# First scores in eight array tiles, and attention placed among the preceding entry's steps, in a fused attention and two-MLP kernel

## The chip, the cores and the metric

The kernel runs on one core of a Trainium2 chip. The metric is the device time of one execution in microseconds (us), the median of three runs. A profiled execution gives the rows; all times are from its trace unless a run is named.

## The reference

Attention in two steps for 8 entries (batch) of 8 heads, 576 tokens and 64 dimensions, with 32 packed queries per head; then an ELU MLP and a second one with SoLU and layer norm. All data are fp32.

```python
def sm_attn(qq, kk, vv):
    s = scale * np.matmul(qq, kk.transpose(0, 1, 3, 2))
    s = s - np.max(s, axis=-1, keepdims=True)
    a = np.exp(s)
    a = a / (np.sum(a, axis=-1, keepdims=True) + 1e-09)
    return np.matmul(a, vv)
p_packed = sm_attn(p, k, v)
out = sm_attn(q, p_packed, p_packed)
...
h = x @ w_in
g = np.where(h > 0.0, h, alpha * (np.exp(np.minimum(h, 0.0)) - 1.0))
return (g @ w_out).astype(np.float32)
```

The second MLP (`_moe2_ref`) multiplies by `w_in2`, takes h times softmax of h, normalises, scales by `g_ln` and multiplies by `w_out2`.

## The kernel before, in words

Weights come as 64-bit words and are narrowed to fp32 on ScalarE and VectorE (`narrow`, four operations per piece of 512 columns); matmuls of the MLPs run in three passes over a high and a low part (`mm3`), so nearly every operand is split into two.

**Attention of entry b.** `s1_mm` gives the first scores (packed queries against k) for a group g of four heads: four matmuls of 128x64, with the packed queries of two heads in a block-diagonal `pt_bd`. `s1_max`, `s1_exp` and `s1_div` are the softmax over 576 keys. For b of 2 and more the probabilities are transposed by `t1_blocks` (32x32 blocks on VectorE) and `t1_move`, 16 block copies per group into `a_sb`; entries 0 and 1 use TensorE (`t1_mm`). `pp_mm` multiplies by v, a group at a time, and `pp_blocks` (16 transposes of 32x32 for both groups) lays the packed values out as `ppT`. `s2_mm` gives the second scores of a half of the tokens, in eight 64x32 tiles of the array (`packed_mm`); a chain of VectorE operations and an exponential on ScalarE are its softmax, and `s2_split` makes the operand `AT`.

**M blocks.** `m_mm` multiplies the packed values by `w_in` in advance: M(b, c) for c of 0 to 3, eight matmuls of 64x32 tiles and 512 columns, split by `m_hi` and `m_lo`. Five slots hold them.

**FFN steps.** 256 steps (b, half, f), f of 0 to 15. A step is `ffn_h` (six matmuls of 288 columns, tile `h`, from `AT` and M(b, f // 4)), `ffn_exp` (two ScalarE operations, tile `fe`), `ffn_max` (VectorE), `ffn_split` (`ghi` on ScalarE, `glo` on VectorE) and `ffn_x2` (12 matmuls of 288 columns into `acc`), three steps behind its `h`. The first 48 steps take entries 0 and 1 in groups of four f, with partial sums through DRAM. From about 766 us on the second MLP runs over 36 blocks of 128 tokens, in a fixed order written at the end of the kernel.

**What sets the order.** Every piece is a `node` with an engine, a cost in us, needs, buffers that it takes and gives back, and perhaps a due time. `order()` computes how late each may start from the due times of its readers, then places nodes one by one: of the nodes of an engine that can start within 0.3 us of the first, the one that may wait least. The result is the program order of TensorE, VectorE, ScalarE and the SP queue; each engine then runs in that order. Due times stand on the steps alone (`FIRST_US + STEP_US * n`), so an entry's attention has no due time of its own. One PSUM tile (two banks, tag `misc`) is shared by all of `s1`, `t1`, `pp`, `s2` and M blocks, so each waits until the one before it is emptied. Costs in the tables are constants, such as

```python
a_in = [node(("mv", *x, h), ACT if h in ACT_MOVES else DVE, 0.75, [("eB", *x), prev_pp],
node(("ppt", *x), DVE, 0.25 if b < 2 else 1.3, [("pp", *x)],
```

where `mv` is four block copies. At the start k, v and weights are loaded in the order of the list `first`; p of entry 0 goes through ScalarE's queue.

Of the kernel before, what the change touches and what calls it, by code (L numbers as in the profile page):

```python
# [34 lines left out]
def attention_mlp_kernel(ctx: ExitStack, tc: tile.TileContext, q, k, v, v_tail, p,  # L35
# [172 lines left out]
    def load_p(b, eng):  # L208
        eng.dma_start(out=pt_bd[0:64, :, 0:NP], in_=p[b, 0:64])
        eng.dma_start(out=pt_bd[64:P, :, NP:], in_=p[b, 64:P])  # L210

    def load_k(b, g, tag=None):
        if tag is None:
            t = work.tile([P, 2, S], F32, tag="k", name=f"k{b}_{g}", bufs=1)
        else:
            t = slot(f"k{b}_{g}", [P, 2, 1024], tag, F32)[:, :, 0:S]
        sp.dma_start(out=t, in_=k[b, g])
        kt[b, g] = t

    def load_v(b, g, tag=None):  # L220
        if tag is None:
            t = v_sb
        else:
            t = slot(f"v{b}_{g}", [P, 8, 4 * D], tag, F32)
            nc.gpsimd.memset(t[S - 4 * CH:, 4], 0.0)
        sp.dma_start(out=t[0:CH, 0:4], in_=v[b, g])
# [808 lines left out]
```

## Time and profile before

| what | value |
|---|---|
| runs (median of three) | 1182.26 us (1179.63 to 1182.43) |
| the profiled execution's own time | 1178.58 us |
| its span, first to last instruction | 1176.8 us |
| TensorE (PE) busy | 1117.9 us, 95% |
| VectorE (DVE) busy | 894.4 us, 76% |
| ScalarE (ACT) busy | 718.6 us, 61% |
| mean granted TensorE clock | 0.987 |
| moved by DMA | 111.04 MB, 94 GB/s |

Busy time of TensorE is modelled, since matmuls overlap: the distance between the starts of two matmuls tells more than a duration. PEld is the loading of weights into the array, which runs beside the matmuls. A releaser (`<-`) is the instruction or transfer that ended a wait. The trace's names leave numbers out: `s` is the first scores (from `k`) and the second ones (from `q`), `h` hidden values of a step, `acc` outputs of a step, `pp` packed values before and `ppT` after the transpose.

### The profile page before, as it was taken

The page shows a single profiled execution, that of the slowest core. Times are in us where ns is not written, and L with a number is a line of the kernel's source. Part 1 is how long each engine was busy: PE and PEld are TensorE (multiplying, and loading weights), DVE is VectorE, ACT ScalarE, POOL GpSimd, SP SyncE. Part 2 cuts the span into 40 slices and gives each one's busy share as a digit, 9 for nine tenths or more (in the row PEclk, how much of TensorE's full clock was granted, in tenths as well). Part 3 has the DMA queues.
Part 4 walks back from the last instruction along what each step waited for, and adds up shares of the span by engine and source line. Part 5 has one row for each costly group of instructions (what it writes and reads, how often), then busy time and mean ns, then how long its engine had stood idle before and what let it go on. Part 6 is the DMA issues. An engine that isn't in the chain of part 4 may idle for free.

```text
span 1176.8 us, 20606 instructions
## 1 busy us (share of the span) xinstructions
PE 1117.9 (95%) x7916; PEld 979.5 (83%) x7916; DVE 894.4 (76%) x2022; ACT 718.6 (61%) x1539; POOL 21.3 (2%) x45
## 2 busy tenths in 40 slices
PE   4699999899999999999999999999999999999997
PEld 2478889699799899899889889988888888888885
DVE  4999995858858868767877765478888788788774
ACT  2567765465465565565466465647766766766674
POOL 0000000000000000000000000000000000000000
PEclk7799999999999999999999999999999999999999
DMA  9837332213322412321422151611111111000000
GB/s 328 333 117 235 121 111 82 84 41 113 101 93 72 145 57 97 119 93 62 132 80 90 46 178 59 218 57 54 54 37 54 52 39 54 27 28 19 28 28 36
DMA packets 53554, 111.04 MB, mean 94 GB/s; under 512 B 8400, under 2 KB 27600, under 8 KB 51664
## 3 DMA queue, kind: packets, MB, share of 16 engines
q1 hardware_dynamic: 52912, 109.66, 27.5%
q8 instruction: 62, 1.02, 0.4%
q14 instruction: 36, 0.29, 0.1%
q10 hardware_dynamic: 544, 0.07, 0.0%
HBM read 77.14 MB, written 32.57 MB: 93 GB/s over the span
## 4 chain that ended last, share of the span: by engine, by line
PE 42%; DVE 31%; ACT 14%; issue 7%; DMA 4%; POOL 1%; SPq 0%; ACTq 0%; POOLq 0%; DVEq 0%
PE acc L64 8%; PE acc L66 8%; PE acc L65 8%; ACT lnX L542 6%; PE h L64 5%; PE h L65 5%; PE h L66 4%; DVE lnB L532 4%; DVE a_sb L295 2%; DVE ln L525 2%; PE m L332 2%; DVE z L517 2%; ACT h L520 2%; DVE lnT L151 2%; DVE nm L508 2%
## 5 line engine op out<-in xcount | busy, mean ns | idle before, releaser
L64 PE MATMUL acc<-ghi,wo 128*128 128x288 f32 x1024 | 308.6, 301 | 1.7 <-ACT x L471 0.7
L66 PE MATMUL acc<-glo,wo 128*128 128x288 f32 x1024 | 302.7, 296 | 1.4 <-DVE glo L434 1.4
L65 PE MATMUL acc<-ghi,wo 128*128 128x288 f32 x1024 | 302.2, 295 | 0.0
L64 PEld LDWEIGHTS acc<-ghi,wo 128*128 128x128 f32 x1024 | 191.9, 187 | 30.8 <-ACT fe L419 14.8
L66 PEld LDWEIGHTS acc<-glo,wo 128*128 128x128 f32 x1024 | 192.6, 188 | 2.6 <-DVE glo L434 2.0
L65 PEld LDWEIGHTS acc<-ghi,wo 128*128 128x128 f32 x1024 | 192.6, 188 | 0.0
L559 PE MATMUL o<-wo,lnT 128*128 128x512 f32 (+1 forms) x592 | 185.5, 386 | 5.6 <-ACT lnT L149 5.6
L424 DVE SCALAR_TENSOR_TENSOR fe<-fe,h 128x288 f32<-128x288 f32 x256 | 114.3, 452 | 88.6 <-ACT fe L419 86.0
L418 ACT ACTIVATE fe<-h 128x288 f32<-128x288 f32 x256 | 104.5, 408 | 118.2 <-PE h L66 92.8
L431 ACT CAST ghi<-fe 128x288 fp32r<-128x288 f32 x256 | 109.4, 431 | 105.2 <-DVE fe L424 104.4
L64 PE MATMUL h<-AT,M 128*128 128x288 f32 x512 | 156.0, 305 | 9.7 <-DVE fe L424 8.9
L542 ACT COPY lnX<-lnB 32x256 f32<-32x256 f32 x288 | 116.3, 404 | 78.0 <-DVE lnB L532 65.2
L65 PE MATMUL h<-AT,M 128*128 128x288 f32 x512 | 152.4, 298 | 0.9 <-DVE M L400 0.9
L66 PE MATMUL h<-AT,M 128*128 128x288 f32 x512 | 150.8, 294 | 0.0
L434 DVE TENSOR_TENSOR glo<-fe,ghi 128x288 fp32r<-128x288 f32 x256 | 114.5, 452 | 46.4 <-ACT ghi L431 42.8
L559 PEld LDWEIGHTS o<-wo,lnT 128*128 128x128 f32 x592 | 111.3, 190 | 28.3 <-ACT lnT L149 6.5
L64 PEld LDWEIGHTS h<-AT,M 128*128 128x128 f32 x512 | 96.6, 189 | 27.5 <-DVE fe L424 11.4
L419 ACT ACTIVATE fe<-fe 128x288 f32<-128x288 f32 x256 | 113.8, 445 | 8.0
L561 PE MATMUL o<-wo,lnT 128*128 128x512 f32 (+1 forms) x296 | 113.9, 386 | 0.0
L64 PE MATMUL h<-wi,x2hi 128*128 128x512 f32 x288 | 112.3, 390 | 1.4 <-ACT h L520 1.4
L65 PE MATMUL h<-wi,x2lo 128*128 128x512 f32 x288 | 112.1, 389 | 0.0
L66 PE MATMUL h<-wi,x2hi 128*128 128x512 f32 x288 | 112.0, 389 | 0.0
(98 smaller groups left out, 1581.8 us busy)
## 6 DMA issues: line engine op xcount, KB each, us to landing
k<-in_k SPq DMA_DIRECT2D x16, 576.0 KB, 3.9
q<-in_q SPq DMA_DIRECT2D x16, 576.0 KB, 3.9
x_dram<-x SPq DMA_DIRECT2D x32, 288.0 KB, 2.5
x2raw<-x_dram SPq DMA_DIRECT2D x9, 1024.0 KB, 5.5
out_x<-y SPq DMA_DIRECT2D x35, 256.0 KB, 2.0
raw_wi<-in_w_in SPq DMA_DIRECT2D x8, 1024.0 KB, 9.3
w_dram<-w SPq DMA_DIRECT2D x16, 512.0 KB, 2.7
...
```

The source lines that it names most:

```text
L64: pe.matmul(o, a[0], b[0], start=start, stop=False)
L65: pe.matmul(o, a[1], b[0], start=False, stop=False)
L66: pe.matmul(o, a[0], b[1], start=False, stop=stop)
L418: act.activation(e, o[:, 0:HS], AF.Relu, scale=-1.0)
L419: act.activation(e, e, AF.Exp, scale=-1.0)
L424: dve.scalar_tensor_tensor(out=e, in0=e, scalar=-1.0, in1=o[:, 0:HS], op0=ALU.add, op1=ALU.max)
L431: act.copy(ghi, e)
L434: dve.tensor_tensor(out=glo, in0=e, in1=ghi.bitcast(F32), op=ALU.subtract)
L532: dve.transpose(t, last.pop(("ln", i)))
L542: act.copy(x, y)
L559: pe.matmul(o, t[:, x, kk], w[:, 0, cs], start=x + kk == 0, stop=x == 1 and kk == 7)
L561: pe.matmul(o, t[:, 0, kk], w[:, 1, cs], start=False, stop=False)
```

## The change

- `s1_mm` takes half w of the keys for all eight heads, in eight 64x32 tiles (`heads_mm`, which was `packed_mm`), from a plain `p_sb`. Each half has a maximum per head, and four exponentials of 288 columns per entry write `e1` with their own maximum. `s1_both`, `s1_scale` and `s1_fac` turn the two maxima and sums into one factor per head and half, and `s1_div` applies it.
- k is loaded by halves (two transfers each), v and q into work buffers `k`, `q` and `v` in turn.
- `pp_mm` takes all eight heads in one group; `pp_blocks` is eight transposes of 32x64 in four nodes.
- Block copies are nodes of two copies (cost 0.5), and `a_sb` holds both halves of the heads.
- Attention nodes of entries 2 to 7 get due times within the 32 steps of the entry before (`by`), M blocks too; `ffn_max` gets one, and that of `x2_out` is a step earlier.
- At the start p is loaded first, and the first weights go ahead of v. The memsets of `pt_bd`, `a_sb` and v go.

The diff, cut to its core:

```diff
-    pt_bd = const.tile([P, 4, 2 * NP], F32, name="pt_bd")
-    a_sb = const.tile([P, 5, P], F32, name="a_sb")
-    v_sb = const.tile([P, 5, 4 * D], F32, name="v_sb")
+    p_sb = const.tile([P, 4, NP], F32, name="p_sb")
+    a_sb = const.tile([P, 5, 2, P], F32, name="a_sb")
...
+    def load_p(b):
+        sp.dma_start(out=p_sb, in_=p[b])
+
+    def load_k(b, half, tag):
+        t = room_for(f"k{b}_{half}", tag)[:, 0:4 * HS].rearrange("p (u t) -> p u t", u=4)
+        for g in range(2):
+            sp.dma_start(out=t[:, 2 * g:2 * g + 2], in_=k[b, g][:, :, half * HS:(half + 1) * HS])
+        kt[b, half] = t
...
-    def s1_mm(b, g, ps2=misc_ps):
-        o = ps2(f"s1_{b}_{g}")
-        kk = kt.pop((b, g))
-        for kh in range(2):
-            for j in range(2):
-                pe.matmul(o[64 * j:64 * j + 64, kh, 0:HS], pt_bd[:, 2 * g + j, :],
-                          kk[:, j, kh * HS:(kh + 1) * HS], start=True, stop=True)
-        st["s1", g] = o
-
-    def s1_max(b, g):
-        nm = small.tile([P, 1], F32, tag="nm", name=f"nm{b}_{g}")
-        dve.tensor_reduce(out=nm, in_=st["s1", g][:, :, 0:HS], axis=AX.XY, op=ALU.max, negate=True)
+    def s1_mm(b, w, ps2=misc_ps):
+
+        o = st["s1", w] = ps2(f"s1_{b}_{w}")
+        heads_mm(o[:, :, 0:HS], p_sb, kt.pop((b, w)))
...
+    def s1_exp(b, w, r):
+
+        if w == 0:
+            st["e1", r] = work.tile([P, S], F32, tag="at", name=f"e1_{b}_{r}", bufs=3)
+        act.activation(st["e1", r][:, w * HS:(w + 1) * HS], st["s1", w][:, r, 0:HS], AF.Exp, scale=0.125,
+                       bias=st["nm"][:, w, r:r + 1], accum_out=st["sm"][:, w, r:r + 1])
...
+    def s1_both(b):
+
+        nm = st["nm"]
+        m = small.tile([P, 1, 2], F32, tag="m1", name=f"m1_{b}")
+        dve.tensor_tensor(out=m, in0=nm[:, 0:1], in1=nm[:, 1:2], op=ALU.min)
+        dve.tensor_tensor(out=nm, in0=m.to_broadcast([P, 2, 2]), in1=nm, op=ALU.subtract)
...
+    def s1_fac(b):
+
+        f, sm = st.pop("nm"), st.pop("sm")
+        dve.tensor_tensor(out=sm, in0=f, in1=sm, op=ALU.mult)
+        r = small.tile([P, 1, 2], F32, tag="r1", name=f"r1_{b}")
+        dve.scalar_tensor_tensor(out=r, in0=sm[:, 0:1], scalar=1e-9, in1=sm[:, 1:2], op0=ALU.add, op1=ALU.add)
+        dve.reciprocal(r, r)
+        dve.tensor_tensor(out=f, in0=f, in1=r.to_broadcast([P, 2, 2]), op=ALU.mult)
+        st["f"] = f
+
+    def s1_div(b, r):
+        e = st["e1", r]
+        for w in range(2):
+            x = e[:, w * HS:(w + 1) * HS]
+            dve.tensor_scalar(out=x, in0=x, scalar1=st["f"][:, w, r:r + 1], scalar2=None, op0=ALU.mult)
...
+        for c in range(5):
+            n = min(CH, S - c * CH)
+            for u1 in range(2):
+                for h in range(4):
+                    u, r = 2 * (h // 2) + u1, h % 2
+                    vv = vt[b, u // 2]
+                    d0 = (2 * (u % 2) + r) * D
+                    pe.matmul(o[h * NP:(h + 1) * NP, u1, 0:D], a_sb[0:n, c, r, u * NP:(u + 1) * NP],
+                              vv[0:n, c, d0:d0 + D], start=(c == 0), stop=(c == 4))
...
+        for x in range(2):
+            n0 = r * D + x * NP
+            dve.transpose(t[n0:n0 + NP, u0:u0 + 2, :], o[h * NP:(h + 1) * NP, :, x * NP:(x + 1) * NP])
...
+            return dict(due=FIRST_US + STEP_US * (32 * (b - 1) + step)) if b > 1 else {}
...
+            k_tag, v_tag, q_tag = ("k", "q"), ("v", "k"), ("q", "k")
...
+                a_in += [node(("mv", b, r, u, j), DVE, 0.5, [("eB", b, r), prev_pp],
+                              lambda r=r, u=u, j=j: t1_move(b, r, u, (j, j + 1)), lets=[eb],
+                              **by(10 + 4 * r + u + j / 4))
+                         for u in range(4) for j in (0, 2)]
...
+                 **by(2.5 + 4 * w))
...
+             takes=[bank], lets=vp, **by(18))
...
+                     **by(18.6 + 0.4 * h))
...
+                        **by(24.5 + 4 * half))
...
+             due=FIRST_US + STEP_US * (32 * (b - 1) + (27, 30, 33, 36.5)[c]) if b > 1 else None)
...
-        node(("fm", *x), DVE, 0.45, [("fx", *x)], lambda: ffn_max(b, half, f), lets=[hp])
+        node(("fm", *x), DVE, 0.45, [("fx", *x)], lambda: ffn_max(b, half, f), lets=[hp], due=due + 2 * STEP_US)
...
-                        dict(lets=[accs_of[i]], takes=[] if again else [xos[i]], due=due + STEP_US * (AHEAD + 1))),
+                        dict(lets=[accs_of[i]], takes=[] if again else [xos[i]], due=due + STEP_US * AHEAD)),
...
-    first = [("k", 0, 0), ("k", 0, 1), ("v", 0, 0), ("v", 0, 1), *raw("wi", 0, 0, 1), ("q", 0, 0), *raw("wo", 0, 0),
-             ("q", 0, 1), ("k", 1, 0), ("p", 1), *raw("wo", 1, 0), ("v", 1, 0), ("k", 1, 1), ("v", 1, 1), ("q", 1, 0),
+    first = [("k", 0, 0), ("k", 0, 1), *raw("wi", 0, 0, 1), ("v", 0, 0), ("v", 0, 1), ("q", 0, 0), *raw("wo", 0, 0),
+             ("q", 0, 1), ("p", 1), ("k", 1, 0), *raw("wo", 1, 0), ("k", 1, 1), ("v", 1, 0), ("v", 1, 1), ("q", 1, 0),
...
-    dve.memset(pt_bd, 0.0)
-    load_p(0, act)
+    load_p(0)
```

**First place: VectorE, the block copies of entry 3** (`a_sb` from `eB3_1`), between step operations of entry 2 (`fe2_1_10` is step 10 of its half 1). Before:

```order
L284 STREAM_TRANSPOSE eB3_1_3671<-e1_3_1_3631 128x576
L295 COPY a_sb_78<-eB3_1_3671 32x5x32 x2
L295 COPY a_sb_78<-eB3_1_3671 32x4x32 x2
L295 COPY a_sb_78<-eB3_1_3671 32x5x32 x2
L295 COPY a_sb_78<-eB3_1_3671 32x4x32 x2
L295 COPY a_sb_78<-eB3_1_3671 32x5x32 x2
L295 COPY a_sb_78<-eB3_1_3671 32x4x32 x2
L295 COPY a_sb_78<-eB3_1_3671 32x5x32 x2
L295 COPY a_sb_78<-eB3_1_3671 32x4x32 x2
L424 SCALAR_TENSOR_TENSOR fe2_1_10_3666<-fe2_1_10_3666,h2_1_10_3634 128x288
```

Now, from the transpose of the first group of heads on:

```order
L296 STREAM_TRANSPOSE eB3_0_3146<-e1_3_0_2986 128x576
L436 SCALAR_TENSOR_TENSOR fe2_0_7_3129<-fe2_0_7_3129,h2_0_7_3101 128x288
L303 COPY a_sb_78<-eB3_0_3146 32x5x32 x2
L446 TENSOR_TENSOR glo2_0_7_3169<-fe2_0_7_3129,ghi2_0_7_3168 128x288
L436 SCALAR_TENSOR_TENSOR fe2_0_8_3160<-fe2_0_8_3160,h2_0_8_3139 128x288
L303 COPY a_sb_78<-eB3_0_3146 32x4x32 x2
L446 TENSOR_TENSOR glo2_0_8_3183<-fe2_0_8_3160,ghi2_0_8_3182 128x288
L303 COPY a_sb_78<-eB3_0_3146 32x5x32 x2
L436 SCALAR_TENSOR_TENSOR fe2_0_9_3197<-fe2_0_9_3197,h2_0_9_3172 128x288
L303 COPY a_sb_78<-eB3_0_3146 32x4x32 x2
L446 TENSOR_TENSOR glo2_0_9_3214<-fe2_0_9_3197,ghi2_0_9_3213 128x288
L303 COPY a_sb_78<-eB3_0_3146 32x5x32 x2
```

The 16 copies stood in one run ahead of `fe2_1_10`; now they stand in pairs between the `fe` and `glo` of steps 7 to 14 of the half before (7 to 9 shown).

**Second place: VectorE, where M block M0_3 is split** (its low part, the last that step 36, `h0_0_12`, needs). Before:

```order
L469 SCALAR_TENSOR_TENSOR part0_1_0_1607<-acc0_1_8_0_1555,part0_1_0_1607 128x576
L469 SCALAR_TENSOR_TENSOR part0_1_1_1608<-acc0_1_8_1_1556,part0_1_1_1608 128x576
L424 SCALAR_TENSOR_TENSOR fe1_0_9_1656<-fe1_0_9_1656,h1_0_9_1632 128x288
L424 SCALAR_TENSOR_TENSOR fe1_0_10_1684<-fe1_0_10_1684,h1_0_10_1665 128x288
L434 TENSOR_TENSOR glo1_0_9_1691<-fe1_0_9_1656,ghi1_0_9_1690 128x288
L400 SCALAR_TENSOR_TENSOR M0_3_1707<-m0_3_1673,M0_3_1707 128x512 x2
L434 TENSOR_TENSOR glo1_0_10_1713<-fe1_0_10_1684,ghi1_0_10_1712 128x288
L107 TENSOR_SCALAR cv_wo6_0_1660<-cv_wo6_0_1660 128x512
```

Now:

```order
L113 SCALAR_TENSOR_TENSOR cv_wo6_1_1720<-raw_wo_6_929,cv_wo6_1_1720 128x512
L243 TENSOR_REDUCE nm2_1800<-s1_2_0_1699 128x2
L244 TENSOR_SCALAR nm2_1800<-nm2_1800 128x2
L151 TENSOR_TENSOR wo6_1797<-cv_wo6_0_1717,wo6_1797 128x512
L151 TENSOR_TENSOR wo6_1797<-cv_wo6_1_1720,wo6_1797 128x512
L481 SCALAR_TENSOR_TENSOR part1_0_0_1745<-acc1_0_8_0_1723,part1_0_0_1745 128x576
L481 SCALAR_TENSOR_TENSOR part1_0_1_1746<-acc1_0_8_1_1724,part1_0_1_1746 128x576
L107 TENSOR_SCALAR cv_wo7_0_1824<-cv_wo7_0_1824 128x512
L109 SCALAR_TENSOR_TENSOR cv_wo7_0_1824<-raw_wo_7_0_1032,cv_wo7_0_1824 128x512
L412 SCALAR_TENSOR_TENSOR M0_3_1841<-m0_3_1826,M0_3_1841 128x512 x2
L107 TENSOR_SCALAR cv_wo7_1_1836<-cv_wo7_1_1836 128x512
```

`wo6` (conversion and split), the maximum `nm2` of entry 2's first half of scores and a partial sum stood behind M0_3 or much later, and now stand ahead of it; so does the softmax of `s2_1_1`, further up.

**Third place: TensorE, the first rows of the program.** Before:

```order
L243 MATMUL s1_0_0_114<-k0_0_96,pt_bd_77 64x288 x4
L243 MATMUL s1_0_1_121<-k0_1_98,pt_bd_77 64x288 x4
L272 MATMUL t1_0_0_143<-ident_76,e1_0_0_131 128x128 x4
L272 MATMUL t1_0_0_143<-ident_76,e1_0_0_131 64x128
L306 MATMUL pp0_0_156<-a_sb_78,v_sb_79 64x32 x20
L272 MATMUL t1_0_1_189<-ident_76,e1_0_1_153 128x128 x4
L272 MATMUL t1_0_1_189<-ident_76,e1_0_1_153 64x128
L306 MATMUL pp0_1_200<-a_sb_78,v0_1_102 64x32 x20
L332 MATMUL s2_0_0_230<-q0_0_110,ppT0_80 32x288 x8
```

Now:

```order
L345 MATMUL s1_0_0_111<-k0_0_91,p_sb_77 32x288 x8
L345 MATMUL s1_0_1_122<-k0_1_94,p_sb_77 32x288 x8
L285 MATMUL t1_0_0_172<-ident_76,e1_0_0_135 128x128 x4
L285 MATMUL t1_0_0_172<-ident_76,e1_0_0_135 64x128
L285 MATMUL t1_0_1_183<-ident_76,e1_0_1_137 128x128 x4
L285 MATMUL t1_0_1_183<-ident_76,e1_0_1_137 64x128
L314 MATMUL pp0_193<-a_sb_78,v0_0_101 64x32 x20
L314 MATMUL pp0_193<-a_sb_78,v0_1_104 64x32 x20
L345 MATMUL s2_0_0_244<-q0_0_107,ppT0_79 32x288 x8
```

The four 64-column matmuls per group are eight of 32 per half, and both groups' values `pp` are one block behind both transposes.

## Rows read from the trace of the kernel before

**Rows 1.** Windows by stage: length; busy PE, PEld, DVE, ACT, POOL; clock; DMA share, GB/s
```profile
48.30:156.70 108.40, 103.59 (x880) 92.02 (x881) 100.44 (x205) 75.34 (x166) 0.00 (x0) 1.00 0.49 160
156.70:238.80 82.10, 76.19 (x649) 70.29 (x650) 62.69 (x158) 43.97 (x103) 0.00 (x0) 1.00 0.29 88
238.80:691.50 452.70, 441.92 (x3842) 401.58 (x3842) 341.14 (x835) 265.42 (x602) 0.00 (x0) 1.00 0.29 95
```

**Rows 2.** TensorE's timeline, entry 3: start us, us, engine, line, operation, tiles, shapes, count
```profile
270.75 0.29 PE L64 MATMUL acc<-ghi,wo 128*128 128x288 f32 x1
...
272.33 0.29 PE L64 MATMUL h<-AT,M 128*128 128x288 f32 x1
...
273.20 1.19 PE L243 MATMUL s<-k,pt_bd 128*64 128x288 f32 x8
...
274.33 0.40 PE L64 MATMUL acc<-ghi,wo 128*128 128x288 f32 x1
...
302.57 0.77 PE L310 MATMUL pp<-v_sb,a_sb 128*32 128x64 f32 x40
...
313.24 0.72 PE L332 MATMUL s<-q,ppT 64*32 64x288 f32 x16 [0.47 <-issue]
...
317.25 1.09 PE L332 MATMUL m<-wi,ppT 64*32 64x512 f32 x16
```

**Rows 3.** What TensorE waited for, 200 to 690 us: us in total, times, longest
```profile
PE h L64 <- DVE fe L424: 5.3, 6, 1.0
...
PE pp L310 <- DVE ppT L319: 3.1, 1, 3.1
...
PE m L332 <- DVE M L400: 1.0, 3, 0.4
```

**Rows 4.** VectorE's timeline behind the first scores of entry 3
```profile
303.98 3.96 DVE L295 COPY a_sb<-eB 32x160 f32<-32x160 f32 x16
...
308.34 1.78 DVE L319 STREAM_TRANSPOSE ppT<-pp 32x32 f32<-32x32 f32 x8
```

**Rows 5.** Groups by line and form: busy us, mean ns | idle before, releasers
```profile
L319 DVE STREAM_TRANSPOSE ppT<-pp 32x32 f32<-32x32 f32 x96 | 20.3, 212 | 1.2
...
L349 DVE STREAM_TRANSPOSE u<-s 128x288 f32<-128x288 f32 x32 | 13.5, 461 | 0.1
...
L418 ACT ACTIVATE fe<-h 128x288 f32<-128x288 f32 x256 | 104.5, 408 | 118.2 <-PE h L66 92.8 <-DVE glo L434 24.7
...
L256 ACT ACTIVATE e<-s,nm 128x576 f32<-128x576 f32 x16 | 11.8, 740 | 16.8 <-DVE nm L250 16.8
...
L256 ACT ACTIVATION_READ_ACCUMULATOR e<-s,nm 128x1 f32 x16 | 3.1, 193 | 0.0
...
L109 DVE SCALAR_TENSOR_TENSOR cv_wo<-raw_wo,cv_wo 128x512 uint32<-128x512 uint32 x24 | 16.5, 687 | 0.3
...
L373 DVE TENSOR_TENSOR u<-u,s2r 128x576 f32<-128x576 f32 x16 | 12.1, 759 | 0.5
```

**Rows 6.** Timelines of TensorE and ScalarE at the start, and the loads of k
```profile
9.87 0.75 PE L243 MATMUL s<-k,pt_bd 128*64 128x288 f32 x2 [9.87 <-DMA pt_bd<-in_p]
...
17.36 0.67 ACT L105 ACTIVATE cv_wi<-raw_wi 128x512 f32<-128x512 f32 x1
...
k<-in_k SPq DMA_DIRECT2D x16, 576.0 KB, 3.9
```

**Rows 7.** Windows at the start (all engines), and of VectorE alone from 98.7 us
```profile
0.00:10.00 10.00, 0.13 (x2) 0.16 (x4) 0.45 (x3) 1.49 (x2) 1.25 (x8) 1.00 0.80 255
...
10.00:20.00 10.00, 7.50 (x66) 5.37 (x66) 4.51 (x14) 3.26 (x7) 0.00 (x0) 0.82 1.01 399
...
98.70:176.00 77.30, 72.24 (x144) 1.00 0.45 140
```

**Rows 8.** Timelines of VectorE and TensorE where M0_3 is ready
```profile
148.71 0.69 DVE L400 SCALAR_TENSOR_TENSOR M<-m,M 128x512 fp32r<-128x512 f32 x1 [0.66 <-ACT M L396]
...
149.88 0.29 PE L64 MATMUL h<-AT,M 128*128 128x288 f32 x1
```

More of the change, by code (lines that the diff above doesn't have):

```diff
@@ L206, in attention_mlp_kernel, with room_for @@
     mt, at = {}, {}
[L208 to L226, printed above, removed]
+    def room_for(name, tag):
+        if tag in ("k", "q", "v"):
+            return work.tile([P, 5 * 4 * D], F32, tag=tag, name=name, bufs=1)
+        return slot(name, [P, 2048], tag, F32)
@@ L284, in t1_blocks, with t1_b, t1_move @@
+    def t1_b(b, r):
+        dve.tensor_copy(a_sb[0:S - 4 * CH, 4, r], st["t1", r][0:S - 4 * CH, 1, 0:P])
+    def t1_blocks(b, r):
+        e = st.pop(("e1", r))
+        t = work.tile([P, S], F32, tag="at", name=f"eB{b}_{r}", bufs=3)
         dve.transpose(t, e)
[L285 to L289 removed]
+        st["eB", r] = t.rearrange("p (c n) -> p c n", n=NP)
+    def t1_move(b, r, u, js):
+        t = st["eB", r]
+        for j in js:
@@ new lines, in attn_nodes @@
+            k_tag, v_tag, q_tag = ("k", "q"), ("v", "k"), ("q", "k")
+        early = [("back", b - 1, 1)] if b else []
+        kp = [(k_tag[w], ("k", b, w)) for w in range(2)]
+        vp = [(v_tag[g], ("v", b, g)) for g in range(2)]
+        es = [("at", ("e", b, r)) for r in range(2)]
+        if b:
+            node(("p", b), SP, 0.4, [("s1", b - 1, 1)], lambda: load_p(b), size=0.1)
+        for w in range(2):
+            node(("k", b, w), SP, 0.8, [], lambda w=w: load_k(b, w, k_tag[w]), takes=[kp[w]], size=0.6)
@@ new lines, in attn_nodes @@
+        for w in range(2):
+            acc = b == 0 and w == 1
+            bank = ("acc" if acc else "misc", ("s1", b, w))
+            node(("s1", b, w), PE, 2.0 if b == 0 else 0.85,
+                 [("p", b) if b else None, ("k", b, w), ("s1", b, 0) if w else None, *early],
+                 lambda w=w, acc=acc: s1_mm(b, w, acc_ps if acc else misc_ps), takes=[bank, *([] if w else es)], lets=[kp[w]],
+                 **by(2.5 + 4 * w))
+            node(("max", b, w), DVE, 0.93, [("s1", b, w), ("max", b, 0) if w else None], lambda w=w: s1_max(b, w))
+            for r in range(2):
+                node(("exp", b, w, r), ACT, 0.63, [("max", b, w), ("exp", b, 0, r) if w else None],
+                     lambda w=w, r=r: s1_exp(b, w, r), lets=[bank])
@@ new lines, in attn_nodes @@
+        bank = ("acc" if b == 0 else "misc", ("pp", b))
+        node(("pp", b), PE, 1.8, a_in + [("v", b, g) for g in range(2)], lambda: pp_mm(b, acc_ps if b == 0 else misc_ps),
+             takes=[bank], lets=vp, **by(18))
+        if b < 2:
+            node(("ppt", b, 0), DVE, 0.3, [("pp", b)], lambda: pp_copy(b), lets=[bank])
+        else:
+            for h in range(4):
+                node(("ppt", b, h), DVE, 0.5, [("pp", b)], lambda h=h: pp_blocks(b, h), lets=[bank],
+                     **by(18.6 + 0.4 * h))
@@ L713, in m_nodes @@
         bank, mp = ("misc", ("m", *x)), (m_slot(b, c), ("M", *x))
-        node(("m", *x), PE, 1.35, [("ppt", b, 0), ("ppt", b, 1), *(("cvG", "wi", c, u) for u in range(4))],
-             lambda: m_mm(b, c), takes=[bank, mp], lets=[(f"wi{c}", c)] if b == B - 1 else [])
+        node(("m", *x), PE, 1.35, [*ppt_of(b), *(("cvG", "wi", c, u) for u in range(4))],
+             lambda: m_mm(b, c), takes=[bank, mp], lets=[(f"wi{c}", c)] if b == B - 1 else [],
+             due=FIRST_US + STEP_US * (32 * (b - 1) + (27, 30, 33, 36.5)[c]) if b > 1 else None)
         for g in range(2):
```

177 lines of the change are left out of this document (66 added, 111 removed).

## The prediction, made before the change was run

> **What bounds the kernel now.** I read the windows by stage first [rows 1]. From 48 us on TensorE is busy 93 to 98% of every stretch and its granted clock is 1.00, so the span is TensorE's own work plus its gaps; VectorE is busy 93% up to 156.7 us, 75 to 76% in the two stretches behind. Counted in the timeline, the output matmuls of step 36 start at 156.7 us, those of step 64 at 238.8, those of step 224 at 691.5. The long middle, 160 steps or five entries, is therefore 452.7 us.
>
> Next, the timeline of TensorE inside that middle, to price its work by starts, since busy times overlap [rows 2]. The 12 output matmuls of a step take 1.58 us (270.75 to 272.33); at the same pace its six hidden ones take 0.79 and end at 273.12, and the insertion behind them starts at 273.20. A step costs 2.39 us with its seams. The first scores of one head group take 1.19 us, a packed-values group 0.77, the second scores of a half 0.72, an M block 1.09. Each insertion costs some 0.12 us more: 0.08 before it and 0.10 in the slower first matmul behind it (0.40 at 274.33, otherwise 0.30), less the 0.06 by which that one overlaps it. Per entry: 32 steps 76.5, insertions 2x1.19 + 2x0.77 + 2x0.72 + 4x1.09 = 9.7, ten seams 1.2, together 87.4. Measured: 452.7/5 = 90.5. So 3.1 us per entry are gaps.
>
> The waits say where the gaps are [rows 3]: TensorE waits for VectorE, for `fe` and for the transposed packed values. The timeline of VectorE says why [rows 4]: 16 block copies run for 3.96 us in one piece, and an `fe` that TensorE's next step needs stands behind them; then come eight small transposes, 1.78 us. The written order has them there (first place shown above), because it was made with 0.75 us for four copies, and the row gives 0.99.
>
> **Steady entries (steps 64 to 224).** The new first scores are eight 64x32 tiles per half, the form, columns and order of the second scores, so I take 0.72 us for each half: 2x(1.19-0.72) = 0.94 us saved, and one seam fewer, 0.12, since the packed values are one group; its 40 matmuls are the two groups of before joined, 2x0.77. An entry then costs 86.3 us of TensorE. The upper end for a half is no gain from the tiles, 1.19; nothing in the rows points there.
>
> The gaps: the order now puts two block copies at a time between the steps' `fe` and `glo`, from 11 steps ahead on, and the transposes three steps ahead of their readers. The longest piece of VectorE work between two `glo` rows falls, by the durations in the rows, from the 16 copies with a division and a transpose before them and eight transposes behind, some 8 us, to under 4 us. Of VectorE's work per entry, 16 transposes of 212 ns [rows 5] become 8 of twice the width. Their price lies between 212 ns (same count of columns) and 424 (two of the old); I take 240, near the low end, since nine times the columns (128x288) cost only 461 [rows 5]; that saves 1.5 us. The divisions are cut in four, and six one-column operations replace four; I set this between 0 and the same 1.5, so VectorE's work per entry stays or falls a little. ScalarE gets four exponentials of 288 columns for two of 576: 4x(0.41+0.19) against 2x(0.74+0.19), +0.5 [rows 5], and a tiny one, 0.2; it is busy 59% of the middle [rows 1], and its idle time hides that. If the cover fails, it shows in the shared bank, below. I leave 0.8 us of gaps per entry, bounds 0 and 2.7 (nine insertions at 0.3): 90.5 - 86.3 - 0.8 = 3.4 us, times five = **-17** (-21 to -7.5).
>
> A row against this: the one shared PSUM bank. Every insertion takes it, and the next has to wait until it is emptied. A first-scores bank is now emptied by a maximum of 0.75 us and two exponentials of 0.60, where one exponential took 0.93, and there are M blocks 2 to 3 us behind it. The Trainium skill, "TensorEngine Tiling (Array Packing)", section Performance Considerations (PSUM Bottleneck), says that tiling speeds up TensorE but not the emptying of PSUM, which may become the bound; by that rule the steady part would be the loss of the second rival, 1194 us in place of 1158. No row of before shows the bank waiting long: TensorE waited for `M` 1.0 us in three times, 0.4 at most [rows 3]; so I go by the rows.
>
> **The start, up to step 64.** Three things move.
> (a) First scores began at 9.87 us, released by the landing of `pt_bd` [rows 6], whose small pieces were queued from ScalarE behind k. Now p is one load, ahead of k, and only half of k is needed. A load of k took 3.9 us from issue to landing, so the first matmul comes between 4.6 and 9.9; I take 6. The weights of the first M block now go ahead of v: p, k and one piece are 2.3 MB, 9 us at the 255 GB/s of the first ten us [rows 7], so their conversion starts near 10.5 instead of 17.36 [rows 6]. VectorE has little else to do there (0.45 and 4.5 us of ten). The chain of softmax gets longer by the common maximum, its exponential and the factors, about 1.2 us. Gain 3.5 us, between 0 and 7.
> (b) Entry 2's attention is spread into steps 35 to 59, where VectorE is 93% busy (98.7 to 176 us) [rows 7]. What decides is M0_3, without which step 36 can't start. It was ready at 149.4, and step 36 began at 149.88 [rows 8]: no slack. In the new order (second place above) it has more in front of it: the softmax of a half of second scores (five operations of 0.76 and two small ones, 4.2), two units of `wo6` (six operations of 0.69, two of 0.42: 5.0), two partial sums (1.5), a maximum (0.9), part of `wo7` (1.1) and the rest of step 35 (1.4), the two sizes from [rows 5], some 14 us of durations, 12.6 after the overlap of neighbours. VectorE's own gaps up to there, 7 of the 8.0 us to 156.7 [rows 1], may take up part; I take half. So M0_3 is ready at 149.4 + 12.6 - 3.5 - 3.5 = 155. TensorE has by then run empty, and step 36's output matmuls follow four us behind (its hidden matmuls 0.8, four element-wise operations of 0.4 to 0.5, and conversions of `wo7` between them on VectorE): 159, 2.3 later than before.
> (c) From there to step 64: 28 steps 66.9, and one half of first scores, the packed values, two halves of second scores and three M blocks with their seams 7.8, gaps 1.5: 76.2 instead of 82.1. The 3.1 us that TensorE once waited for `ppT` [rows 3] are among what goes.
> Together **-3.5** (-10.5 to +3.5, by the bounds of a and b).
>
> **The end.** One M block (M7_1) and the last second scores leave the stretch behind step 224 for earlier ones, where they are counted: 1.09 + 0.72 + 2x0.12 = 2.05, and a gap of 0.5: **-2.5** (-4 to 0). From step 254 on the order of all engines is the same in both; the last stage's work buffers only change size. POOL's memsets of v go; nothing on the path waited for them. SP issues one load of p instead of two and four of k instead of two; their readers stand steps behind them, except at the start, which is counted in (a).
>
> **Sum.** 3.5 + 17 + 2.5 = 23 us off the profiled execution's 1178.6 gives 1155.6. That execution was 3.7 us under the median of the runs, 1182.3; I add some two thirds of it and forecast **1158 us**.
>
> **Rivals.**
> 1. The start eats its gain: nothing of (a) arrives and no gap of VectorE takes up the 12.6 us. Then step 36's outputs come 9.3 later, the start is +3.3, the sum -16.2: 1165 us with the median's offset. For it: 93% busy, and M0_3 without slack. Against: ten us without VectorE work at the start.
> 2. Slower: the single bank. Nine insertions per entry stand in TensorE's queue in program order, and steps behind them wait too. If each waits 0.9 us for the bank (a maximum of 0.75 and one of the two exponentials not hidden by what stands between), gaps are 8.1 per entry in place of 0.8: the middle becomes 5x(8.1 - 4.2) = 19.5 slower, the sum with the start and end as forecast +13.5, and 1194 us. It decides from a mean wait of 0.6 per insertion on: there 5x(5.4 - 4.2) eats the 6.0 of start and end. Against: the waits for `M` in [rows 3].
> 3. A milder form, 0.3 us each: the middle gives 7.5, and 1167 us.
> 4. The tiles of the first scores don't run side by side: the 0.94 us of six entries are lost, 1164. The second scores speak against it.
> 5. The start gains its full 10.5: 1151.
>
> **Chances.** Forecast 0.60; rival 1 0.14; 2 0.06; 3 0.12; 4 0.02; 5 0.06. The range 1146 to 1173 leaves out rival 2, and tails of the others. A measurement of this kernel tells about 0.3% (3.5 us) from no change: faster 0.91, the same 0.04, slower 0.05 (most of rival 2).
>
> **What would show it.** First scores: 8-matmul blocks of 0.72 us. Copies on VectorE in pairs, none longer than 0.5 us. Step 64's outputs start near 235 us, step 224's near 671, so 436 for the middle. First scores start near 6 us. M0_3 near 155. I am wrong if the middle takes over 445 us, if TensorE waits for the bank (`s`, `m` from `M`, `e`) over 2 us per entry, or if step 64 comes after 240.

## The result, and the profile after

The changed kernel takes **1160.08 us** (median of 4 runs, 1159.38 to 1161.45) against 1180.95 for the kernel before in the same session: ratio 0.9825, 95% interval 0.9806 to 0.9843. The forecast was 1158 with 1146 to 1173. The profiled execution spans 1158.2 us.

First the changed kernel's page: busy time by engine, the granted clock in 40 slices, and the chain of waits.

```profile
PE 1112.3 (96%) x8044; PEld 977.5 (84%) x8044; DVE 885.6 (76%) x2002; ACT 723.4 (62%) x1579; POOL 20.4 (2%) x42
...
PEclk9999999999999999999999999999999999999998
...
PE 52%; DVE 24%; ACT 13%; issue 6%; DMA 2%; POOL 1%; SPq 0%; POOLq 0%; ACTq 0%; DVEq 0%
```

TensorE, VectorE and ScalarE were busy 1117.9, 894.4 and 718.6 us before. The totals moved by 1% or less; what moved is when TensorE stands idle. The windows by stage answer to [rows 1]; they are cut where the output matmuls of steps 0, 36, 64 and 224 start. Columns: stretch, length, busy PE, PEld, DVE, ACT, POOL, clock, DMA share, GB/s.

```profile
47.10:166.40 119.30, 109.28 (x906) 96.35 (x900) 109.14 (x227) 78.13 (x174) 0.00 (x0) 0.96 0.55 185
166.40:243.60 77.20, 75.67 (x681) 69.39 (x681) 59.60 (x147) 44.99 (x105) 0.00 (x0) 1.00 0.25 77
243.60:675.50 431.90, 431.75 (x3923) 396.82 (x3922) 332.97 (x815) 266.86 (x628) 0.00 (x0) 1.00 0.30 100
```

| stretch (starts of output matmuls) | before | after | change | forecast |
|---|---|---|---|---|
| span's start to step 36 | 156.7 | 166.4 | +9.7 | +2.3 |
| steps 36 to 64 | 82.1 | 77.2 | -4.9 | -5.9 |
| steps 64 to 224 | 452.7 | 431.9 | -20.8 | -17 |
| step 224 to the end | 485.3 | 482.7 | -2.6 | -2.5 |
| span | 1176.8 | 1158.2 | -18.6 | -23 |

In the middle TensorE is busy in 431.75 of 431.90 us, and the waits of TensorE from 200 to 690 us have no row at all, where [rows 3] had `fe`, `ppT` and `M`. Its timeline in entry 3's stretch answers to [rows 2] (start us, us, engine, line, operation, tiles, shapes, count).

```profile
255.43 0.72 PE L345 MATMUL s<-k,p_sb 64*32 64x288 f32 x16
256.07 0.40 PE L64 MATMUL acc<-ghi,wo 128*128 128x288 f32 x1
...
284.14 1.46 PE L325 MATMUL pp<-v,a_sb 128*32 128x64 f32 x80
...
291.30 0.71 PE L345 MATMUL s<-q,ppT 64*32 64x288 f32 x16
...
308.89 1.09 PE L345 MATMUL m<-wi,ppT 64*32 64x512 f32 x16
```

A half of the first scores takes 0.72 us, as the second scores do, and the next matmul starts 0.64 behind its start. On VectorE, in the same stretch, the copies now stand in pairs (sometimes two pairs) between `fe` and `glo`; [rows 4] had 3.96 us in one piece.

```profile
262.39 0.46 DVE L446 TENSOR_TENSOR glo<-fe,ghi 128x288 fp32r<-128x288 f32 x1 [0.27 <-ACT ghi L443]
262.77 0.45 DVE L436 SCALAR_TENSOR_TENSOR fe<-fe,h 128x288 f32<-128x288 f32 x1
263.25 0.45 DVE L303 COPY a_sb<-eB 32x128 f32<-32x128 f32 x2
263.73 0.46 DVE L446 TENSOR_TENSOR glo<-fe,ghi 128x288 fp32r<-128x288 f32 x1
264.22 0.51 DVE L303 COPY a_sb<-eB 32x160 f32<-32x160 f32 x2
...
285.67 2.06 DVE L337 STREAM_TRANSPOSE ppT<-pp 32x64 f32<-32x64 f32 x8 [0.30 <-PE pp L325]
```

The start is the stretch that got longer. VectorE's timeline in front of M0_3 answers to [rows 8]:

```profile
155.86 0.45 DVE L446 TENSOR_TENSOR glo<-fe,ghi 128x288 fp32r<-128x288 f32 x1
156.23 0.68 DVE L113 SCALAR_TENSOR_TENSOR cv_wo<-raw_wo,cv_wo 128x512 uint32<-128x512 uint32 x1
156.83 0.75 DVE L243 TENSOR_REDUCE nm<-s 128x2 f32<-128x576 f32 x1
157.62 0.17 DVE L244 TENSOR_SCALAR nm<-nm 128x2 f32<-128x2 f32 x1
157.69 1.29 DVE L151 TENSOR_TENSOR wo<-cv_wo,wo 128x512 fp32r<-128x512 f32 x2
158.90 1.42 DVE L481 SCALAR_TENSOR_TENSOR part<-acc,part 128x576 f32<-128x576 f32 x2
160.23 0.42 DVE L107 TENSOR_SCALAR cv_wo<-cv_wo 128x512 uint32<-128x512 uint32 x1
160.69 0.69 DVE L109 SCALAR_TENSOR_TENSOR cv_wo<-raw_wo,cv_wo 128x512 uint32<-128x512 uint32 x1
161.48 1.29 DVE L412 SCALAR_TENSOR_TENSOR M<-m,M 128x512 fp32r<-128x512 f32 x2
```

The second half of M0_3 ends at 162.8 us; before it was 149.4. The rows in front, a weight conversion, a maximum of entry 2's first scores, `wo6`, two partial sums and the first of `wo7`, follow each other almost without a gap.

The startup moved but brought nothing. Timelines of the changed kernel, answering to [rows 6]:

```profile
4.63 1.87 PE L345 MATMUL s<-k,p_sb 64*32 64x288 f32 x16 [4.63 <-DMA k<-in_k]
...
11.32 0.66 ACT L105 ACTIVATE cv_wi<-raw_wi 128x512 f32<-128x512 f32 x1 [2.62 <-DMA raw_wi<-in_w_in]
...
19.94 5.48 PE L314 MATMUL pp<-a_sb,v 128*64 128x32 f32 x78 [0.64 <-ACT a_sb L288]
...
25.46 0.29 DVE L329 COPY ppT<-pp 128x128 f32<-128x128 f32 x1 [3.70 <-PE pp L314]
```

The first matmul came 5.2 us earlier and the conversion 6.0, near the forecast (6 us, and 10.5 for the conversion). But the packed values of all heads are one group of 80 matmuls behind the softmax of both halves; before, the first group's 40 ran beside the second group's softmax. The copy `ppT` waits 3.70 us for them in VectorE's queue, with conversions behind it. Up to 36 us VectorE had done 19.2 us of work, before 18.9, and step 0's outputs start at 47.1 us, before at 47.3.

### The profile page after: what moved, and what is told of

The parts are those of the page before. It is cut to its first block, busy times and chain, and to the rows that moved or that the text cites. A ratio compares the mean times of both kernels' runs of the same rounds, so it can differ in the third digit from the quotient of the medians.

```text
span 1158.2 us, 20789 instructions
## 1 busy us (share of the span) xinstructions
PE 1112.3 (96%) x8044; PEld 977.5 (84%) x8044; DVE 885.6 (76%) x2002; ACT 723.4 (62%) x1579; POOL 20.4 (2%) x42
## 4 chain that ended last, share of the span: by engine, by line
PE 52%; DVE 24%; ACT 13%; issue 6%; DMA 2%; POOL 1%; SPq 0%; POOLq 0%; ACTq 0%; DVEq 0%
PE acc L64 10%; PE acc L66 10%; PE acc L65 10%; ACT lnX L554 6%; PE h L64 6%; PE h L65 5%; PE h L66 5%; DVE lnB L544 4%; DVE ln L537 2%; PE m L345 2%; DVE z L529 2%; ACT h L532 2%; DVE lnT L151 2%; DVE nm L520 2%; PE s L345 2%
## 5 line engine op out<-in xcount | busy, mean ns | idle before, releaser
L64 PE MATMUL h<-AT,M 128*128 128x288 f32 x512 | 156.6, 306 | 8.1 <-DVE fe L436 5.1
L64 PEld LDWEIGHTS h<-AT,M 128*128 128x128 f32 x512 | 96.8, 189 | 33.4 <-DVE fe L436 11.0
```

What stands on the lines that cost most here:

```text
L64: pe.matmul(o, a[0], b[0], start=start, stop=False)
```

## Experiments

Times by step are read from each run's timeline. "The middle" is steps 64 to 224. "The change" is the changed kernel; where nothing else is said it is what was edited.

**E1. Entry 2 without due times.**

```diff
-            return dict(due=FIRST_US + STEP_US * (32 * (b - 1) + step)) if b > 1 else {}
+            return dict(due=FIRST_US + STEP_US * (32 * (b - 1) + step)) if b > 2 else {}
...
-             due=FIRST_US + STEP_US * (32 * (b - 1) + (27, 30, 33, 36.5)[c]) if b > 1 else None)
+             due=FIRST_US + STEP_US * (32 * (b - 1) + (27, 30, 33, 36.5)[c]) if b > 2 else None)
```

> Edit: entry 2's attention and M blocks get no due times; entries 3 to 7 keep theirs. Theory (spreading entry 2 into steps 35 to 59 is what cost the start: 12.6 us of VectorE's work stand ahead of M0_3): M0_3 is back behind the work that stood ahead of it before, the output matmuls of step 36 start at 156 to 160 us instead of 166.4, those of step 64 at 235 to 240 instead of 243.6, the middle (steps 64 to 224) stays at 431.9 within 2, and the time falls by 4 to 9 us to 1151 to 1156. Rival A (the late step 36 comes from the startup's own order, which this edit leaves alone): step 36 stays at 164 or later, 1160 within 2. Rival B (the work is only moved: what leaves the place ahead of M0_3 is missing before step 64): step 36 at 156 to 160, step 64 at 243 or later, 1160 within 2.

1162.13 us (1161.08 to 1164.9), ratio 0.9836 (0.9807 to 0.9866): no gain over the change. Step 36 starts at 156.6, step 64 at 243.7: rival B. M0_3 is ready at 149.3 again, so entry 2's due times are what kept it back. (Not all of the 9.8 us at step 36 is theirs: 1.3 stand at step 4 already, up to which both runs have the same order. From 50 to 70 us the granted clock was 1.00 here and 0.91 in the change.) Without due times entry 2's divisions, transposes and copies came in one piece. VectorE's timeline:

```profile
211.06 1.21 DVE L278 TENSOR_SCALAR e<-e,nm 128x288 f32<-128x288 f32 x4
212.18 1.59 DVE L296 STREAM_TRANSPOSE eB<-e 128x576 f32<-128x576 f32 x2
213.69 7.91 DVE L303 COPY a_sb<-eB 32x160 f32<-32x160 f32 x32
221.63 0.46 DVE L446 TENSOR_TENSOR glo<-fe,ghi 128x288 fp32r<-128x288 f32 x1
```

What TensorE waited for from 150 to 245 us (total, times, longest):

```profile
PE pp L325 <- DVE a_sb L303: 8.0, 4, 3.5
```

The 9.8 us that step 36 gained, 14.5 by step 57, are gone by step 62: step 57 alone takes 13.9 us instead of 2.4.

**E2. The old order of the first loads (v ahead of the first weights).**

```diff
-    first = [("k", 0, 0), ("k", 0, 1), *raw("wi", 0, 0, 1), ("v", 0, 0), ("v", 0, 1), ("q", 0, 0), *raw("wo", 0, 0),
+    first = [("k", 0, 0), ("k", 0, 1), ("v", 0, 0), ("v", 0, 1), *raw("wi", 0, 0, 1), ("q", 0, 0), *raw("wo", 0, 0),
```

> Edit: the first loads in the order of before: v ahead of the first weights. Theory (the startup is set by the chain softmax, transposes, packed values of 5.5 us, ppT; v is not what it waits for, and the conversion of the weights on ScalarE stands ahead of the second half's exponentials): ppT is ready 0 to 2 us earlier than 25.5, conversions of wi0 start 3 to 6 us later, step 0 and step 36 move by less than 2, time 1160 within 2.5. Rival (the load order carries the gain that the start has kept): step 36 5 us later or more, time 1164 or more.

1162.06 us, ratio 0.9829 (0.9806 to 0.9851): the theory in the main. The packed values end 0.9 us earlier and the first conversion starts 3.8 later; step 0 comes at 49.2, step 36 at 167.6, 1.3 later. The new load order carries nothing of the time that can be told from noise.

**E3. The kernel before with the planner's costs put right, no due times.**

```diff
-                a_in = [node(("mv", *x, h), ACT if h in ACT_MOVES else DVE, 0.75, [("eB", *x), prev_pp],
+                a_in = [node(("mv", *x, h), ACT if h in ACT_MOVES else DVE, 1.0, [("eB", *x), prev_pp],
-            node(("ppt", *x), DVE, 0.25 if b < 2 else 1.3, [("pp", *x)],
+            node(("ppt", *x), DVE, 0.25 if b < 2 else 1.8, [("pp", *x)],
```

> Edit: the kernel before with the planner's costs put right: 1.0 us for four block copies instead of 0.75, 1.8 for eight transposes instead of 1.3; no due times. The prediction said that the lump of copies stands there because the order was made with 0.75. Theory of the prediction (wrong costs made the lumps): the middle falls by 5 us or more from 452.7, time 1177 or less. Rival (the lumps come from missing due times; the written order still has a piece of 7.5 us per entry): middle 449 to 456, time within 3 us of before.

1183.07 us, ratio 1.0011 (1.0000 to 1.0022); middle 455.3: the rival. The prediction gave the wrong cost as the reason for the lump; it is not.

**E4. No due times for any entry's attention.**

```diff
-            return dict(due=FIRST_US + STEP_US * (32 * (b - 1) + step)) if b > 1 else {}
+            return dict(due=FIRST_US + STEP_US * (32 * (b - 1) + step)) if b > 9 else {}
```

and the M blocks the same.

> Edit: no due times for the attention and the M blocks of any entry; tiles of the first scores, the one group of packed values and the pairs of copies stay. By the written order VectorE then has one piece per entry of some 12.0 us between two glo (both divisions, both transposes, 32 copies), where the kernel before had 7.1 and 3.1 us of gaps per entry. Theory (the spreading took the gaps away; the tiles alone are worth some 1.1 us per entry): gaps of 3 to 8 us per entry come back, the middle takes 447 to 472 us instead of 431.9, step 36 starts near 158, the time is 1168 to 1195. Rival (tiles and the one group carry the gain, the spreading little): middle at most 440, time 1160 or less.

1224.57 us, ratio 1.0359 (1.0334 to 1.0384): slower than the kernel before, and worse than either theory. The middle takes 492.2 us, 12.1 per entry more than the change. What TensorE waited for from 250 to 665 us, in which four entries' packed values lie:

```profile
PE pp L325 <- DVE a_sb L303: 33.4, 16, 3.5
```

Windows around one of the four places (columns as above):

```profile
400.00:410.00 10.00, 9.08 (x79) 8.21 (x77) 6.24 (x19) 5.41 (x15) 0.00 (x0) 1.00 0.33 118
410.00:420.00 10.00, 2.62 (x63) 1.93 (x64) 9.37 (x37) 0.80 (x2) 0.00 (x0) 0.58 0.01 2
420.00:430.00 10.00, 10.00 (x100) 8.43 (x91) 6.60 (x18) 3.46 (x8) 0.00 (x0) 0.74 0.58 185
430.00:440.00 10.00, 10.00 (x95) 8.56 (x80) 9.50 (x20) 7.65 (x17) 0.00 (x0) 1.00 0.12 47
```

The packed values stand in TensorE's queue ahead of steps that were ready, and wait for 32 copies: 33.4/4 = 8.4 us. Some 3.7 of the 12.1 remain: in the stretch of the wait and the next one the granted clock is 0.58 and 0.74, so the matmuls behind the wait are slower. So the spreading is no refinement of the joined group but its condition: joined and unspread, both halves' copies fall together.

**E5. First scores of entries 2 to 7 twice, into the same bank.**

```diff
-        heads_mm(o[:, :, 0:HS], p_sb, kt.pop((b, w)))
+        kk = kt.pop((b, w))
+        for _ in range(2 if b > 1 else 1):
+            heads_mm(o[:, :, 0:HS], p_sb, kk)
```

> Edit: the change's kernel with the first scores of entries 2 to 7 computed twice into the same bank (eight matmuls more per half, the second time over the first; the result is the same). Theory (TensorE bounds the middle without a gap, so its work counts one for one): 2 x 0.646 us more per entry, middle 431.9 + 6.5 = 438.4 (437.5 to 439.5), time up by 7.8 (six entries) to 1167 to 1169. This is also what the tiles are worth turned round: before, a half took 1.12 us, with two of 0.646 it takes 1.29. Rival (idle time or the bank hides part of it): middle below 436, time below 1165.

1163.36 us (1161.22 to 1164.57), ratio 0.985 (0.9827 to 0.9872); the middle is 436.5, 4.6 more. TensorE's timeline in this run:

```profile
253.79 1.20 PE L347 MATMUL s<-k,p_sb 64*32 64x288 f32 x32
254.92 0.40 PE L64 MATMUL acc<-ghi,wo 128*128 128x288 f32 x1
```

The next matmul starts 1.13 behind the first, in the change 0.64: eight more tiles cost 0.49, not 0.646, since the seam (some 0.15) is paid once. Ten halves give 4.9, measured 4.6, between theory and rival: the middle counts TensorE's work nearly one for one, and the price in the theory was off. By the medians 3.3 to 3.5 us came through, a time as the rival has it. Entry 2's two halves stand ahead of step 36's outputs, where TensorE waits for VectorE anyway. And the profiled execution reached step 36 2.1 us earlier than the change's with the same order on VectorE and ScalarE; its granted clock was 1.00 from 50 to 70 and from 140 to 160 us, the change's 0.91 in both.

**E6. The planner told what entry 0's packed values cost.**

```diff
-        node(("pp", b), PE, 1.8, a_in + [("v", b, g) for g in range(2)], lambda: pp_mm(b, acc_ps if b == 0 else misc_ps),
+        node(("pp", b), PE, 1.8 if b > 1 else 5.6, a_in + [("v", b, g) for g in range(2)], lambda: pp_mm(b, acc_ps if b == 0 else misc_ps),
```

> Edit: the planner counts 5.6 us instead of 1.8 for the packed values of entries 0 and 1 (the row shows 5.48 for 78 of the 80 matmuls). The written order then puts two conversion operations ahead of the copy ppT, for which VectorE stood idle 3.7 us. Theory (startup's gain was lost in that wait, with VectorE bound from there on): step 0's outputs 1 to 3 us earlier than 47.1, step 36 the same amount earlier, time 1157 to 1159.5. Rival (step 36 is set by what stands ahead of M0_3 in VectorE's queue later on, or the conversions wait for landings): 1160 within 1.5.

1160.70 us, ratio 0.9822 (0.9795 to 0.985). Step 0's outputs come at 40.5 us, 6.6 earlier, yet step 4's at 67.9 (67.5 in the change) and step 36's at 165.1, 1.3 earlier. So the time is the rival's. From 50 to 150 us VectorE is busy 94.0 of 100: it is what is late, not the first step.

**E7. Entry 2's due times pressed into its last 20 steps.**

```diff
-            return dict(due=FIRST_US + STEP_US * (32 * (b - 1) + step)) if b > 1 else {}
+            return dict(due=FIRST_US + STEP_US * (32 * (b - 1) + (step if b > 2 else 12 + step * (32 - 12) / 32))) if b > 1 else {}
...
-             due=FIRST_US + STEP_US * (32 * (b - 1) + (27, 30, 33, 36.5)[c]) if b > 1 else None)
+             due=FIRST_US + STEP_US * (32 * (b - 1) + ((27, 30, 33, 36.5) if b > 2 else (29, 31.5, 34, 36.5))[c]) if b > 1 else None)
```

> Edit: entry 2's due times are kept but pressed into the last 20 of its 32 steps (step s of the entry becomes 12 + s x 20/32; M blocks 29, 31.5, 34, 36.5). E1 showed that with nothing of entry 2 ahead of M0_3 step 36 starts at 156.6 us, and that the work it left undone then stands in one piece at steps 57 to 59 and costs the same 10 us. In the new order M0_3 stands where it stood before and no piece between two glo of steps 48 to 64 is over 4 us. Theory (VectorE has room between steps 44 and 64 for entry 2's work if it is spread there): step 36's outputs at 156 to 158 us, those of step 64 at 233 to 237 instead of 243.6, middle 432 within 1.5, time 1149 to 1154. Rival (VectorE is the bound from step 0 to step 64 whatever the order, so that step 64 can't come earlier than its work allows): step 64 at 241 or later, 1158 to 1162.

1155.03 us (1153.03 to 1158.56), ratio 0.9779 (0.9754 to 0.9804): between theory and rival. In the profiled execution step 36's outputs come at 160.8 and step 64's at 242.8, as the rival has it. But up to 70 us its written order is E1's, and it had already lost 4.2 us to E1 by step 4. Windows of E7, then of E1:

```profile
50.00:70.00 20.00, 18.36 (x180) 15.53 (x179) 13.43 (x34) 8.60 (x19) 0.00 (x0) 0.74 0.67 258
```

```profile
50.00:70.00 20.00, 18.21 (x206) 15.34 (x205) 17.42 (x42) 11.98 (x26) 0.00 (x0) 1.00 0.75 286
```

The granted clock was 0.74 there, TensorE got 26 matmuls less done in the same busy time, and VectorE behind it 4 us less. By subtraction, without those 4.2 us step 36 would be at 156.6, as in E1, and step 64 at 238.6. Between the two steps E7 takes 81.9 us, for 87.0 in E1 and the theory's 77 to 79; E8 shows where the rest is.

**E8. E7 and E6 together.**

> Edit: that of the run before, and the planner counts 5.6 us for the packed values of entries 0 and 1 (E6). E6 brought step 0 forward by 6.6 us and step 36 by 1.3, and step 64 by 1.5. Theory (startup matters little since VectorE is the bound up to step 36): 0 to 2 us less than the run before. Rival (with the wait ahead of M0_3 gone, startup's gain comes through in full): 4 us or more less.

1153.53 us (1151.73 to 1155.37), ratio 0.9763 (0.9743 to 0.9784); 1.5 less than E7, intervals overlapping. Steps 36 to 64 take 80.9 us: at step 48 a division, a transpose and a partial sum stand together on VectorE, TensorE waits 0.8 and 1.0 us, and the window 185 to 200 us shows the clock at 0.89. Step 48 takes 5.2 us, as in E7.

**E9. The kernel before, spread.** Due times like the change's on the old nodes, `ffn_max` and `x2_out` among them; entry 2's attention is pressed as in E7, its M blocks are not. Copies are planned in pairs and a group's transposes at 1.8 us. The first scores in 128x64 tiles and the two groups stay.

```diff
+                 lets=[kp], **by(2.5 + 7.5 * g))
...
+                     takes=[("at", ("eB", *x))], lets=[("at", ("e", *x))], **by(5.5 + 7.5 * g))
+                a_in = [node(("mv", *x, h, j), DVE, 0.5, [("eB", *x), prev_pp],
+                             lambda g=g, h=h, j=j: t1_move(b, g, h, (j, j + 1)),
+                             lets=[("at", ("eB", *x))], **by(6 + 7.5 * g + h + j / 4)) for h in range(4) for j in (0, 2)]
...
```

> Edit: the kernel before (first scores in 128x64 tiles by groups of heads, packed values in two groups) with due times like the change's, entry 2's pressed as in E7, and the block copies planned in pairs. Theory (the spreading takes the gaps away, the tiles and the one group take 2 x 0.475 us and a seam of 0.12 per entry): no gaps in the middle, 431.9 + 5 x 1.07 = 437.2 (436 to 440), step 64 within 2 us of E7's plus 1, the time 6 to 8 us above E7's, some 1157 to 1161. Rival (the two groups with one buffer for k can't be spread, the joining was needed for it): middle at 444 or more, time 1165 or more.

1158.87 us (1157.92 to 1160.48), ratio 0.981 (0.979 to 0.9829), 3.8 above E7. The window of the middle:

```profile
238.60:677.10 438.50, 437.89 (x3841) 400.77 (x3841) 337.48 (x835) 264.78 (x603) 0.00 (x0) 1.00 0.30 98
```

438.5 us, against 452.7 unspread and 431.9 in the change: **of the middle's 20.8 us the spreading is worth 14.2 and the tiles with the joined group 6.6.** That split holds where the old form is spread; with the joined group the spreading is worth 60.3 (E4). E9's middle is 6.8 longer than E7's, yet its profiled span only 1.1: E9 is 1.7 earlier at step 36, 2.5 shorter from there to step 64, which the theory did not expect, and 1.5 shorter behind step 224. Only the 1.7 can be E7's start with the lower clock; 1.9 of the 2.5 are E7's step 48 (5.2 us, here 3.3); the 1.5 stay open. Spread, the old form is as fast as the change, though entry 2 is pressed here and not in the change.

**E10 and E11. E8, with entry 2 pressed into the last 16 and 18 steps.**

```diff
-            return dict(due=FIRST_US + STEP_US * (32 * (b - 1) + (step if b > 2 else 12 + step * (32 - 12) / 32))) if b > 1 else {}
+            return dict(due=FIRST_US + STEP_US * (32 * (b - 1) + (step if b > 2 else 16 + step * (32 - 16) / 32))) if b > 1 else {}
```

In E11 the 16 is 14, which leaves 18 steps.

> Edit: as E8, with entry 2's due times pressed into the last 16 of its 32 steps instead of 20. E8 lost some 3.5 us at step 48, where a division, a transpose and the partial sum of step 48 came in one piece of 5.6 us between two glo, and the granted clock fell to 0.91 behind it. Here no piece of steps 36 to 55 is over 4.0 us, the one of step 50 is 3.0. Theory (pieces over some 4 us stop TensorE, and the order can avoid them): steps 36 to 64 take 77.5 to 79 us instead of 80.9, time 1 to 3 us under E8's: 1150 to 1153. Rival (the same work later meets the second scores of entry 2, pieces of 4.9 and 5.6 at steps 57 and 61, and stops TensorE there): 36 to 64 at 80 to 82, 1153 to 1156.

E10: **1151.64 us** (1151.09 to 1152.23), ratio 0.9749 (0.9736 to 0.9762). Its windows, cut at the outputs of steps 0, 36, 64 and 224:

```profile
40.50:154.60 114.10, 104.55 (x896) 93.94 (x889) 107.56 (x226) 80.29 (x178) 0.00 (x0) 0.99 0.62 207
154.60:234.50 79.90, 77.36 (x706) 69.28 (x707) 64.92 (x160) 44.60 (x108) 0.00 (x0) 1.00 0.34 102
234.50:666.20 431.70, 431.58 (x3922) 396.73 (x3921) 332.58 (x814) 267.15 (x628) 0.00 (x0) 1.00 0.30 99
```

What its TensorE waited for from 195 to 212 us:

```profile
PE h L64 <- DVE fe L436: 1.7, 3, 1.1
```

Step 36 starts at 154.6, 2.1 before the kernel before and 11.8 before the change; step 64 at 234.5, 9.1 before the change. Its 36 to 64, 79.9 us, lies between the two expectations: the stop at step 48 is gone, 1.7 us of waits for `fe` are left.

Not all of the early step 36 is due to the order. E8, E10 and E11 have the same order on TensorE, VectorE and ScalarE up to step 40, yet step 36 is at 157.2 in E8 and E11, and the 2.7 us stand at step 4 already (70.2 there, 67.5 in E10). E8, then E10:

```profile
55.00:65.00 10.00, 8.58 (x116) 7.59 (x122) 8.05 (x18) 5.22 (x11) 0.00 (x0) 0.84 0.80 321
```

```profile
55.00:65.00 10.00, 8.51 (x129) 7.19 (x128) 9.28 (x21) 5.73 (x13) 0.00 (x0) 1.00 0.79 315
```

The granted clock was 0.84 in E8 and E11 and 1.00 in E10. What the 16 steps themselves give against 20 and 18 is in steps 36 to 64: 1.0 and 1.7 us.

> Edit: as E8, with 18 steps instead of 20. Pieces of 4.2 and 3.8 us at steps 50 and 51, of 5.6 at steps 57 and 61. Theory as for the run before, with a little less room: 36 to 64 take 78 to 80 us, 1150.5 to 1153.5. Rival: as there.

E11: 1153.59 us, ratio 0.9767 (0.9754 to 0.9781); 36 to 64 takes 81.6, the rival's value. Whether 16 steps beat 18 and 20 in the total is not shown, since the 2.7 us of the start are in it.

**E12. The change again, beside E10 and E11.**

> The changed kernel as it is, timed beside the two candidates below and the kernel before on one chip. Expected: 1160 within 2, and 2.4 us of difference or more to both candidates. Its first 100 us may differ by some us from its first profile, if the granted clock of that stretch is another.

1159.86 us (1159.41 to 1164.86), ratio 0.9834 (0.9814 to 0.9854); step 36 at 166.4, step 64 at 243.7, as in its first profile. So the late step 36 belongs to the order but for some 2 us that go with the clock (E5: 164.2). E10, 8.2 us below and with step 4 at the same time as here (67.5), beats both kernels.

## Why the prediction was right, and where it was wrong

**The steady entries** were right in sign, place and mechanism: the middle got 20.8 us shorter, 3.8 more than forecast and just inside the bound of 21. The tiles and the seam were put at 5x(0.94 + 0.12) = 5.3 and are 6.6 with the joined group (E9). The rest of the 17, some 11.7, was for the gaps (2.3 of 3.1 per entry); they gave 14.2 (E9): the 0.8 left over per entry were too many, there are none. The price of a half of first scores, 0.72, holds row for row, that of the wider transposes (240 ns) nearly: eight take 2.06 us. The **reason** that the prediction gave for the lumps, the planner's 0.75, fell (E3): what was missing is a due time (E4, E9).

**The bank** did not bind: rivals 2 and 3 have no row in the middle. With nine insertions per entry through one PSUM tile TensorE has no wait for it there; in this order steps stand between the insertions. The Trainium skill, "TensorEngine Tiling (Array Packing)", section Performance Considerations (PSUM Bottleneck), says that emptying PSUM may become the bound; this trace does not show it.

**The start failed, and rival 1 is what happened.** The forecast was -3.5 up to step 64; it was +4.8. The step that failed is the absorption: (a) took 3.5 us of gain from the earlier first matmul, and (b) let VectorE's own gaps swallow another 3.5 of the 12.6 us in front of M0_3. Neither came: M0_3 is ready at 162.8, where 149.4 + 12.6 = 162.0 is the sum without absorption, and step 36's outputs are 9.7 later, where rival 1 said 9.3. Step 64 at 243.6 is past the 240 that the prediction itself named as a sign of being wrong. (a) failed because an earlier first matmul gives VectorE no more work done by 36 us (19.2 against 18.9), the joined packed values being in the way; E6 shows further that even a step 0 that is 6.6 us earlier is used up by step 4. The sum of durations in front of M0_3 was right: with that work gone, in E1, M0_3 is ready at 149.3 and step 36's outputs come 9.8 us earlier, 1.3 of which go with the clock before step 4. Part (c), 77.2 for a forecast of 76.2, was right.

**The end** was right, -2.6 for -2.5. The time, 2 us over the forecast, is so near because the steady part's 3.8 us more pay for half of the 8.3 that the start fell short. That the two errors had opposite signs is luck.

**Open.** E10 left 1.7 us of waits for `fe` behind step 52. In how many executions the clock before step 4 is full is not known, so the part of it in the medians is open. Whether the start can be shortened by taking work off VectorE was not tried.
